# Two heads' k'v in one chain of 128-row matmuls on a block-diagonal v, with v cast by GpSimd and 26 warm-up matmuls

## The chip, the cores and the metric

The kernel runs on one core of one Trainium2 chip. Its engines are TensorE (PE in the profile, with its weight loads as PEld), VectorE (DVE), ScalarE (ACT), GpSimd (POOL) and SyncE (SP), which issues most DMAs. The metric is the device time of one execution in microseconds (us); the median of several runs counts. About 2% of it is a difference that a measurement of this kernel can tell.

## The reference

Eight batches, eight heads, 576 positions, head dimension 64. A linear attention with cosine and sine features is followed by a small token-mixing network on the 512-wide result:

```python
q_p = phi(q, cos_w, sin_w)          # relu(x)*cos, relu(x)*sin: 128 features
k_p = phi(k, cos_w, sin_w)
kv = np.einsum('bhsf,bhsd->bhfd', k_p, v)
z = np.sum(k_p, axis=2)
num = np.einsum('bhsf,bhfd->bhsd', q_p, kv)
den = np.einsum('bhsf,bhf->bhs', q_p, z)[..., None] + 1e-06
x = num / den                       # heads side by side: [B, S, 512]
wq = x @ w_q
wk = x @ w_k
W_tok = scale * np.einsum('bsd,btd->bst', wq, wk)
mixed = np.einsum('bst,btd->bsd', W_tok, x)
out = np.maximum(mixed, 0.0) @ w_out
```

Inputs and output are float32; the kernel's matmuls take bfloat16.

## The kernel before

Everything is unrolled. For each batch, `attention` runs over four pairs of heads, then `moe_front` makes the mixed matrix, and after each second batch `wout` multiplies 1152 rows by w_out and stores them.

A pair of heads is loaded so that head 0 lies on partitions 0 to 63 and head 1 on 64 to 127; each partition holds nine positions (C9 = 9). Loads come in halves of a batch (two pairs), in quarters for the first batch. `kf`, `vf` and `qf` (two buffers each) are the loaded floats. ACT or DVE makes `rk` and `rq` by a relu (line 121) and casts v into `v_ext` (line 116); GpSimd sets a column of ones in `v_ext` (line 119), which gives z beside kv. DVE multiplies `rk` and `rq` by the table `cossin` into `k_p` and `q_p` (line 123).

Per pair PE does two chains of nine matmuls into `kv_ps` (line 136), one per head, each on the 64 partitions of its head, with 128 features as weights and 65 columns of v. `kv_ps` has one bank, and each chain is copied to `kv_sb` (line 144) by ACT or DVE. Between the two chains stand nine transposes of `q_p` into `qpt_ps` (line 147), which DVE copies to `qpt_sb` (line 151). Then ten matmuls give `num_ps` (line 159), DVE takes the reciprocal (line 167) and writes the quotient to `x_sb` (line 168, three buffers).

`moe_front` transposes `x_sb` (`xT_ps`, line 180), multiplies by w_q and w_k (`moe_ps_a`, line 191), transposes a part (`moe_ps_b`), forms `moe_ps_c` (line 213, five matmuls of 512 columns) and `moe_ps_d` (line 226), which ACT or DVE evicts into `mix_sb` (line 233). `wout` fills `moe_ps_e` (line 244), copies it to `o_sb` (line 252) and stores it. All `moe_ps` tiles share three banks.

The order on each engine is made by a scheduler ahead of the run, from the program's order, priorities (`high_priority` for the evictions) and estimated costs; `nc.any` lets it choose between ACT and DVE. It lets the attention of later batches run ahead of the network of earlier ones. Each engine, and SP's queue, then works through its own list in order.

Of the kernel before, what the change touches and what calls it, by code (L numbers as in the profile page):

```python
# [14 lines left out]
FP32 = mybir.dt.float32  # L15
BF16 = mybir.dt.bfloat16
# [6 lines left out]
def kernel(  # L23
# [10 lines left out]
    nc = tc.nc  # L34

    B, H, S, D = q.shape
    DM = H * D
    DH = moe_w_q.shape[1]
    P = 128
    NPAIR = H // 2  # L40
    C9 = (2 * S) // P
# [4 lines left out]
    consts = ctx.enter_context(tc.tile_pool(name="consts", bufs=1))  # L46
    inp = ctx.enter_context(tc.tile_pool(name="inp", bufs=2))
    work = ctx.enter_context(tc.tile_pool(name="work", bufs=2))
    small = ctx.enter_context(tc.tile_pool(name="small", bufs=6))
    xpool = ctx.enter_context(tc.tile_pool(name="xpool", bufs=3))  # L50
    moepool = ctx.enter_context(tc.tile_pool(name="moepool", bufs=2))
    mixpool = ctx.enter_context(tc.tile_pool(name="mixpool", bufs=2))
    outpool = ctx.enter_context(tc.tile_pool(name="outpool", bufs=4))
    psum = ctx.enter_context(tc.tile_pool(name="psum", bufs=1, space=bass.MemoryType.PSUM))

    ident = consts.tile([P, P], BF16)
    make_identity(nc, ident)
# [31 lines left out]
    wo_sb = consts.tile([P, NDM, DM], BF16)  # L89
    nc.vector.tensor_copy(wo_sb, wo_f)  # L90

    num_slices = [(i * P, P) for i in range(4)] + [(S - P, P)]
    cbase_of = [0, 2, 4, 6, 7]
    xread_slices = [(i, 0, P, i * P) for i in range(4)] + [(4, 64, 64, 4 * P)]

    def attention(b, x_sb, nsplit):
        qf = inp.tile([P, NPAIR, C9 * D], FP32, name="qf")
        kf = inp.tile([P, NPAIR, C9 * D], FP32, name="kf")
        vf = inp.tile([P, NPAIR, C9 * D], FP32, name="vf")
        rq = work.tile([P, NPAIR, C9, D], BF16, name="rq")  # L100
        rk = work.tile([P, NPAIR, C9, D], BF16, name="rk")
        q_p = work.tile([P, NPAIR, C9, 2, D], BF16, name="q_p")
        k_p = work.tile([P, NPAIR, C9, 2, D], BF16, name="k_p")
        v_ext = work.tile([P, NPAIR, C9, D + 1], BF16, name="v_ext")

        step = NPAIR // nsplit
        for sp in range(nsplit):
            a, bb = sp * step, (sp + 1) * step
            csb = cossin.unsqueeze(1).to_broadcast([P, step, C9, 2, D])
            for dst, rr, pp, src in ((kf, rk, k_p, k), (vf, None, None, v),  # L110
                                     (qf, rq, q_p, q)):
                s4 = src[b].flatten().rearrange(
                    "(pr p e) -> p pr e", pr=NPAIR, p=P)
                nc.sync.dma_start(dst[:, a:bb, :], s4[:, a:bb, :])
                if rr is None:
                    nc.any.tensor_copy(  # L116
                        v_ext[:, a:bb, :, 0:D],
                        dst[:, a:bb, :].rearrange("p pr (c d) -> p pr c d", c=C9))
                    nc.gpsimd.memset(v_ext[:, a:bb, :, D:D + 1], 1.0)
                else:  # L120
                    nc.any.tensor_scalar(rr[:, a:bb, :, :], dst[:, a:bb, :],  # L121
                                         0.0, None, op0=ALU.max)
                    nc.vector.tensor_mul(  # L123
                        pp[:, a:bb, :, :, :],
                        rr[:, a:bb, :, :].unsqueeze(3).to_broadcast(
                            [P, step, C9, 2, D]),
                        csb)

        for pr in range(NPAIR):
            kv_sb = small.tile([P, 2, D + 1], BF16, name="kv_sb")  # L130
            qpt_ps = psum.tile([P, C9, P], BF16, name="qpt_ps", bufs=1)
            for hh in range(2):
                p0 = hh * 64
                kv_ps = psum.tile([P, D + 1], FP32, name="kv_ps", bufs=1)
                for c in range(C9):
                    nc.tensor.matmul(  # L136
                        kv_ps,
                        k_p[p0:p0 + 64, pr, c, :, :],
                        v_ext[p0:p0 + 64, pr, c, :],
                        start=(c == 0),  # L140
                        stop=(c == C9 - 1),
                    )
                with tc.high_priority(2000):
                    nc.any.tensor_copy(kv_sb[:, hh, :], kv_ps)  # L144
                if hh == 0:
                    for c in range(C9):
                        nc.tensor.transpose(  # L147
                            qpt_ps[:, c, :], q_p[:, pr, c, :, :], ident)
            qpt_sb = small.tile([P, 2, C9, D], BF16, name="qpt_sb")
            with tc.high_priority(2000):  # L150
                nc.vector.tensor_copy(  # L151
                    qpt_sb, qpt_ps.rearrange("f c (hh pp) -> f hh c pp", hh=2))

            for hh in range(2):
                h = 2 * pr + hh
                num_ps = psum.tile([P, SC, D + 1], FP32, name="num_ps", bufs=2)
                for u in range(SC):
                    cb = cbase_of[u]
                    nc.tensor.matmul(  # L159
                        num_ps[:, u, :],  # L160
                        qpt_sb[:, hh, cb:cb + 2, :],
                        kv_sb[:, hh, :],
                        start=True,
                        stop=True,
                    )
                rec = small.tile([P, SC, 1], FP32, name="rec")
                nc.vector.reciprocal(rec, num_ps[:, :, D:D + 1])
                nc.vector.tensor_tensor(  # L168
                    x_sb[:, :, h, :],
                    num_ps[:, :, 0:D],  # L170
                    rec.to_broadcast([P, SC, D]),
                    op=ALU.mult,
                )
# [129 lines left out]
```

## Time and profile before

| | us |
|---|---|
| median of 3 runs | 202.64 |
| fastest and slowest run | 201.63, 207.41 |
| span of the profiled execution | 206.3 |
| PE busy | 168.7 (82%) |
| DVE busy | 136.7 (66%) |
| ACT busy | 101.0 (49%) |
| GpSimd busy | 2.7 (1%) |

The profile is of one execution; for it the page gives the span from the first to the last instruction. Busy times of PE include the latency of its pipeline, so two matmuls that follow each other overlap in the record: what a chain costs is read from the start of one chain to the start of the next. The chain of waits follows the work that ended last backwards from the last instruction. The granted clock is the share of 2.4 GHz that TensorE was given; 0.50 is 1.2 GHz.

### The profile page before, as it was taken

What the parts mean: (1) busy time and instruction counts of PE and PEld (TensorE: products, weight loads), DVE (VectorE), ACT (ScalarE), POOL (GpSimd) and SP (SyncE); (2) the same over time, 40 slices, a digit from 0 to 9 for tenths busy, and PEclk for the clock granted to TensorE, in tenths of its full rate; (3) what the DMA queues carried; (4) which work ended last, traced back from release to release, by engine and by line L of the source; (5) the groups of instructions that cost most, each with busy time, mean ns of one, the idle gap of its engine ahead of it and who ended that gap; (6) DMA issues with size and microseconds to landing.
All of it is one profiled execution on the core that took longest, in us unless ns stands there. A gap on an engine that the chain in (4) does not pass through costs nothing.

```text
span 206.3 us, 4215 instructions
## 1 busy us (share of the span) xinstructions
PE 168.7 (82%) x1696; PEld 102.8 (50%) x1696; DVE 136.7 (66%) x301; ACT 101.0 (49%) x190; POOL 2.7 (1%) x25
## 2 busy tenths in 40 slices
PE   0007889899789999999979999999799999778950
PEld 0006677555445534866645555766554575532420
DVE  1269667945877468978886898878989497723000
ACT  2174579063923645525834858239645434114540
POOL 2000000000000000000000000000000000000000
PEclk9999999999999999999755999999999999965896
DMA  6999999999500028789995066891003870000486
GB/s 189 381 358 332 401 391 391 389 341 327 198 0 2 0 54 201 165 257 394 394 391 216 0 153 147 189 362 72 3 0 80 204 180 2 3 0 0 105 204 149
DMA packets 20514, 39.32 MB, mean 191 GB/s; under 512 B 3088, under 2 KB 3088, under 8 KB 20496
## 3 DMA queue, kind: packets, MB, share of 16 engines
q1 hardware_dynamic: 18912, 37.76, 58.1%
q10 hardware_dynamic: 1584, 1.31, 2.0%
q8 instruction: 13, 0.21, 0.5%
q14 instruction: 5, 0.04, 0.1%
HBM read 29.62 MB, written 9.44 MB: 189 GB/s over the span
## 4 chain that ended last, share of the span: by engine, by line
PE 67%; DVE 10%; DMA 9%; ACT 7%; issue 2%; SPq 1%; POOL 0%; ACTq 0%; DVEq 0%
PE moe_ps_e L244 14%; PE kv_ps L136 12%; PE qpt_ps L147 11%; PE num_ps L159 7%; PE xT_ps L180 6%; DMA kf<-in_k_dram 6%; PE moe_ps_c L213 6%; PE moe_ps_a L191 6%; PE moe_ps_d L226 4%; DMA wq_f<-in_moe_w_q_dram 2%; DVE x_sb L168 2%; ACT mix_sb L233 2%; DVE qpt_sb L151 1%; DVE xT_sb L185 1%; DVE k_p L123 1%
## 5 line engine op out<-in xcount | busy, mean ns | idle before, releaser
L136 PE MATMUL kv_ps<-v_ext,k_p 64*128 64x65 bf16 x576 | 38.5, 211 | 18.9 <-DVE k_p L123 16.3
L136 PEld LDWEIGHTS <-k_p 64*128 64x128 bf16 x576 | 27.7, 106 | 29.1 <-DVE k_p L123 16.3
L244 PE MATMUL moe_ps_e<-wo_sb,mix_sb 128*128 128x512 bf16 x144 | 35.9, 410 | 0.4 <-ACT o_sb L252 0.3
L147 PE MATMUL qpt_ps<-ident,q_p 128*128 128x128 bf16 x288 | 31.8, 254 | 0.2 <-DVE qpt_sb L151 0.2
L168 DVE TENSOR_TENSOR x_sb<-num_ps,rec 128x320 bf16<-128x320 f32 x64 | 30.1, 482 | 0.1
L151 DVE COPY qpt_sb<-qpt_ps 128x1152 bf16<-128x1152 bf16 x32 | 24.2, 756 | 7.0 <-PE qpt_ps L147 6.6
L144 ACT CAST kv_sb<-kv_ps 128x65 bf16<-128x65 f32 x44 | 9.5, 216 | 36.4 <-PE kv_ps L136 35.7
L159 PE MATMUL num_ps<-kv_sb,qpt_sb 128*128 128x65 bf16 x320 | 24.0, 214 | 1.8 <-DVE x_sb L168 1.4
L252 ACT COPY o_sb<-moe_ps_e 128x512 f32<-128x512 f32 x31 | 18.2, 586 | 14.5 <-PE moe_ps_e L244 9.5
L244 PEld LDWEIGHTS <-mix_sb 128*128 128x128 bf16 x144 | 14.7, 104 | 19.1 <-issue 5.6
L147 PEld LDWEIGHTS <-q_p 128*128 128x128 bf16 x288 | 21.1, 113 | 4.1 <-issue 1.7
L180 PE MATMUL xT_ps<-ident,x_sb 128*128 128x128 bf16 (+1 forms) x160 | 19.5, 243 | 4.2 <-DVE x_sb L168 4.2
L121 ACT ACTIVATE rk<-kf 128x1152 bf16<-128x1152 f32 (+1 forms) x17 | 18.4, 1081 | 7.5 <-DMA kf<-in_k_dram 5.7
L123 DVE TENSOR_TENSOR k_p<-rk,cossin 128x2304 bf16<-128x2304 bf16 (+1 forms) x18 | 21.8, 1213 | 0.0
L123 DVE TENSOR_TENSOR q_p<-rq,cossin 128x2304 bf16<-128x2304 bf16 (+1 forms) x18 | 21.8, 1212 | 0.0
L159 PEld LDWEIGHTS <-qpt_sb 128*128 128x128 bf16 x320 | 16.9, 109 | 9.4 <-issue 3.1
L233 ACT ACTIVATE mix_sb<-moe_ps_d 128x64 bf16<-128x64 f32 (+1 forms) x40 | 14.7, 409 | 9.7 <-PE moe_ps_d L226 8.8
L121 ACT ACTIVATE rq<-qf 128x1152 bf16<-128x1152 f32 (+1 forms) x17 | 18.5, 1086 | 1.7 <-DMA qf<-in_q_dram 1.7
L226 PE MATMUL moe_ps_d<-wqkT_sb,kx_sb 64*128 64x512 bf16 x64 | 16.7, 341 | 2.4 <-ACT mix_sb L233 1.5
L233 DVE TENSOR_SCALAR mix_sb<-moe_ps_d 128x512 bf16<-128x512 f32 (+1 forms) x24 | 11.2, 475 | 10.0 <-PE moe_ps_d L226 9.7
L116 ACT CAST v_ext<-vf 128x1152 bf16<-128x1152 f32 (+1 forms) x16 | 17.5, 1103 | 0.0
L180 PEld LDWEIGHTS <-x_sb 128*128 128x128 bf16 (+1 forms) x160 | 12.2, 108 | 10.4 <-DVE x_sb L168 4.7
(40 smaller groups left out, 106.1 us busy)
## 6 DMA issues: line engine op xcount, KB each, us to landing
out_dram<-o_sb SPq DMA_DIRECT2D x72, 128.0 KB, 2.3
kf<-in_k_dram SPq DMA_DIRECT2D x14, 576.0 KB, 10.0
vf<-in_v_dram SPq DMA_DIRECT2D x14, 576.0 KB, 9.4
qf<-in_q_dram SPq DMA_DIRECT2D x14, 576.0 KB, 9.6
kf<-in_k_dram SPq DMA_DIRECT2D x4, 288.0 KB, 5.1
vf<-in_v_dram SPq DMA_DIRECT2D x4, 288.0 KB, 5.7
qf<-in_q_dram SPq DMA_DIRECT2D x4, 288.0 KB, 6.0
wo_f<-in_moe_w_out_dram ACTq DMA_DIRECT2D x1, 1024.0 KB, 9.9
```

Of the source, the lines that this page charges most:

```text
L121: nc.any.tensor_scalar(rr[:, a:bb, :, :], dst[:, a:bb, :], 0.0, None, op0=ALU.max)
L123: nc.vector.tensor_mul(pp[:, a:bb, :, :, :], rr[:, a:bb, :, :].unsqueeze(3).to_broadcast([P, step, C9, 2, D]), csb)
L136: nc.tensor.matmul(kv_ps, k_p[p0:p0 + 64, pr, c, :, :], v_ext[p0:p0 + 64, pr, c, :], start=(c == 0), stop=(c == C9 - 1),)
L147: nc.tensor.transpose(qpt_ps[:, c, :], q_p[:, pr, c, :, :], ident)
L151: nc.vector.tensor_copy(qpt_sb, qpt_ps.rearrange("f c (hh pp) -> f hh c pp", hh=2))
L159: nc.tensor.matmul(num_ps[:, u, :], qpt_sb[:, hh, cb:cb + 2, :], kv_sb[:, hh, :], start=True, stop=True,)
L168: nc.vector.tensor_tensor(x_sb[:, :, h, :], num_ps[:, :, 0:D], rec.to_broadcast([P, SC, D]), op=ALU.mult,)
L180: nc.tensor.transpose(xT_ps[:, j0:j0 + npn], x_sb[p0:p0 + npn, u, 2 * hp:2 * hp + 2, :], ident[p0:p0 + npn, p0:p0 + npn],)
L226: nc.tensor.matmul(mx_ps[:, 0:nn], kx_sb[:, dmc * P:(dmc + 1) * P], wqkT_sb[0:64, n0:n0 + nn], start=True, stop=True,)
L233: nc.any.tensor_scalar(mix_sb[:, dmc, half * S + n0: half * S + n0 + nn], mx_ps[:, 0:nn], scale_moe, 0.0, op0=ALU.mult, op1=ALU.max,)
L244: nc.tensor.matmul(o_ps, mix_sb[:, dmc, rt * P:(rt + 1) * P], wo_sb[:, dmc, :], start=(dmc == 0), stop=(dmc == NDM - 1),)
L252: nc.any.tensor_copy(o_sb, o_ps)
```

## The change

v of a pair is laid out as a block-diagonal matrix: a tile `v_buf0` or `v_buf1` (by the batch's parity) has, for each pair and position, 2 x 65 columns; a head's 64 partitions hold its v and a one in its own 65 columns and zeros in the other head's. Zeros and ones are set once, ahead of the loop, by DVE for the first 64 partitions and by GpSimd for the others. Each v is cast into its block by GpSimd, 64 partitions and one pair at a time (eight casts of 64x576 per batch). One chain of nine matmuls over all 128 partitions, with 130 columns, then gives both heads' kv, and one copy of 128x130 evacuates it. The transposes of q follow the chain in the program. 26 matmuls of 512 columns on a tile of ones open PE's program. `xpool` has two buffers instead of three, and `rq` and `rk` one instead of two.

```diff
-    xpool = ctx.enter_context(tc.tile_pool(name="xpool", bufs=3))
+    xpool = ctx.enter_context(tc.tile_pool(name="xpool", bufs=2))
...
+    warm = consts.tile([P, 512], BF16)
+    nc.vector.memset(warm, 1.0)
+    warm_ps = psum.tile([P, 512], FP32, name="warm_ps", tag="moe", bufs=3)
+    for _ in range(26):
+        nc.tensor.matmul(warm_ps, warm[:, 0:P], warm, start=True, stop=True)
...
+    v_bufs = []
+    for i in range(2):
+        vb = consts.tile([P, NPAIR, C9, 2, D + 1], BF16, name=f"v_buf{i}")
+        for hh in range(2):
+            p0 = hh * 64
+            eng = nc.vector if hh == 0 else nc.gpsimd
+            eng.memset(vb[p0:p0 + 64, :, :, 1 - hh, :], 0.0)
+            eng.memset(vb[p0:p0 + 64, :, :, hh, D:D + 1], 1.0)
+        v_bufs.append(vb)
...
-        rq = work.tile([P, NPAIR, C9, D], BF16, name="rq")
-        rk = work.tile([P, NPAIR, C9, D], BF16, name="rk")
+        rq = work.tile([P, NPAIR, C9, D], BF16, name="rq", bufs=1)
+        rk = work.tile([P, NPAIR, C9, D], BF16, name="rk", bufs=1)
...
-        v_ext = work.tile([P, NPAIR, C9, D + 1], BF16, name="v_ext")
+        v_ext = v_bufs[b % 2]
...
-                    nc.any.tensor_copy(
-                        v_ext[:, a:bb, :, 0:D],
-                        dst[:, a:bb, :].rearrange("p pr (c d) -> p pr c d", c=C9))
-                    nc.gpsimd.memset(v_ext[:, a:bb, :, D:D + 1], 1.0)
+                    for hh in range(2):
+                        p0 = hh * 64
+                        for pr in range(a, bb):
+                            nc.gpsimd.tensor_copy(
+                                v_ext[p0:p0 + 64, pr, :, hh, 0:D],
+                                dst[p0:p0 + 64, pr, :].rearrange(
+                                    "p (c d) -> p c d", c=C9))
...
-            for hh in range(2):
-                p0 = hh * 64
-                kv_ps = psum.tile([P, D + 1], FP32, name="kv_ps", bufs=1)
-                for c in range(C9):
-                    nc.tensor.matmul(
-                        kv_ps,
-                        k_p[p0:p0 + 64, pr, c, :, :],
-                        v_ext[p0:p0 + 64, pr, c, :],
-                        start=(c == 0),
-                        stop=(c == C9 - 1),
-                    )
-                with tc.high_priority(2000):
-                    nc.any.tensor_copy(kv_sb[:, hh, :], kv_ps)
-                if hh == 0:
-                    for c in range(C9):
-                        nc.tensor.transpose(
-                            qpt_ps[:, c, :], q_p[:, pr, c, :, :], ident)
+            kv_ps = psum.tile([P, 2, D + 1], FP32, name="kv_ps", bufs=1)
+            for c in range(C9):
+                nc.tensor.matmul(
+                    kv_ps,
+                    k_p[:, pr, c, :, :],
+                    v_ext[:, pr, c, :, :],
+                    start=(c == 0),
+                    stop=(c == C9 - 1),
+                )
+            with tc.high_priority(2000):
+                nc.any.tensor_copy(kv_sb, kv_ps)
+            for c in range(C9):
+                nc.tensor.transpose(
+                    qpt_ps[:, c, :], q_p[:, pr, c, :, :], ident)
```

The scheduler makes a new order for the changed program. At the beginning of DVE's list, before the first multiplications, stood this:

```order
L84 CAST wqk_sb<-wq_f 128x4x64
L121 TENSOR_SCALAR rk<-kf 128x576
L85 CAST wqk_sb<-wk_f 128x4x64
L116 CAST v_ext<-vf 128x9x64
L121 TENSOR_SCALAR rq<-qf 128x576
L116 CAST v_ext<-vf 128x9x64
L90 CAST wo_sb<-wo_f 128x2048
```

And now:

```order
L57 MEMSET warm 128x512
L104 MEMSET v_buf_144 64x36x65
L90 CAST wqk_sb<-wq_f 128x4x64
L105 MEMSET v_buf_144 64x36
L91 CAST wqk_sb<-wk_f 128x4x64
L104 MEMSET v_buf_149 64x36x65
L105 MEMSET v_buf_149 64x36
L140 TENSOR_SCALAR rq<-qf 128x576
L96 CAST wo_sb<-wo_f 128x2048
```

Five memsets took the place of the first relu of k, which went to ACT, and of two casts of v, which went to GpSimd.

On ACT, the place where `moe_ps_d` of the first batch is evicted (names with their buffer numbers) read, before:

```order
L233 ACTIVATE mix_sb_372<-moe_ps_d_431 128x512
L121 ACTIVATE rk_1184<-kf_1181 128x1152
L144 CAST kv_sb_641<-kv_ps_663 128x65
L233 ACTIVATE mix_sb_372<-moe_ps_d_440 128x64
L233 ACTIVATE mix_sb_372<-moe_ps_d_446 128x64
L116 CAST v_ext_1187<-vf_1182 128x18x64
L233 ACTIVATE mix_sb_372<-moe_ps_d_452 128x64
```

and now:

```order
L161 CAST kv_sb_605<-kv_ps_607 128x130
L249 ACTIVATE mix_sb_366<-moe_ps_d_425 128x512
L249 ACTIVATE mix_sb_366<-moe_ps_d_431 128x512
L249 ACTIVATE mix_sb_366<-moe_ps_d_434 128x64
L249 ACTIVATE mix_sb_366<-moe_ps_d_437 128x512
L249 ACTIVATE mix_sb_366<-moe_ps_d_440 128x64
L249 ACTIVATE mix_sb_366<-moe_ps_d_443 128x512
L249 ACTIVATE mix_sb_366<-moe_ps_d_446 128x64
```

Seven of the batch's eight evictions now stand in a row on ACT, where four stood among other casts and relus. In the whole program ACT has 29 of the 32 evictions of 512 columns (19 before), DVE three (13 before). On PE the first real instructions are now the nine transposes of the first pair, then its kv chain; before, the first kv chain stood ahead of them.

## Rows read from the trace of the kernel before

**Rows 1.** The chain that ended last: shares of the span by engine, by line.

```profile
PE 67%; DVE 10%; DMA 9%; ACT 7%; issue 2%; SPq 1%; POOL 0%; ACTq 0%; DVEq 0%
PE moe_ps_e L244 14%; PE kv_ps L136 12%; PE qpt_ps L147 11%; PE num_ps L159 7%; PE xT_ps L180 6%; DMA kf<-in_k_dram 6%; PE moe_ps_c L213 6%; PE moe_ps_a L191 6%; PE moe_ps_d L226 4%; DMA wq_f<-in_moe_w_q_dram 2%; DVE x_sb L168 2%; ACT mix_sb L233 2%; DVE qpt_sb L151 1%; DVE xT_sb L185 1%; DVE k_p L123 1%
```

**Rows 2.** Stretches: length, busy PE, PEld, DVE, ACT, POOL (instructions), clock, DMA, GB/s.

```profile
16.30:76.50 60.20, 54.77 (x477) 34.74 (x478) 42.90 (x92) 31.46 (x51) 0.52 (x4) 1.00 0.65 236
114.00:182.60 68.60, 63.67 (x760) 39.54 (x755) 55.49 (x124) 35.43 (x82) 0.52 (x4) 1.00 0.41 105
```

**Rows 3.** The chain in order of time: start, length, moe_ps_c's five matmuls.

```profile
64.87 2.41 PE moe_ps_c L213 x5
...
109.98 2.41 PE moe_ps_c L213 x5
...
136.30 1.31 PE moe_ps_c L213 x5
```

**Rows 4.** kv_ps alone on PE: stretch, length, busy (matmuls), clock, DMA, GB/s.

```profile
16.00:76.50 60.50, 14.80 (x189) 1.00 0.65 236
100.40:114.00 13.60, 2.19 (x35) 0.50 0.83 309
```

**Rows 5.** PE in order of time: start, length, engine, line, matmuls.

```profile
19.66 0.68 PE L136 MATMUL kv_ps<-v_ext,k_p 64*128 64x65 bf16 x9
20.27 1.14 PE L147 MATMUL qpt_ps<-ident,q_p 128*128 128x128 bf16 x9
21.34 0.67 PE L136 MATMUL kv_ps<-v_ext,k_p 64*128 64x65 bf16 x9
...
143.79 0.46 PE L136 MATMUL kv_ps<-v_ext,k_p 64*128 64x65 bf16 x9
144.18 0.68 PE L147 MATMUL qpt_ps<-ident,q_p 128*128 128x128 bf16 x9
144.69 0.32 PE L159 MATMUL num_ps<-kv_sb,qpt_sb 128*128 128x65 bf16 x5
```

**Rows 6.** Waits: who waited for whom, us in total, times, longest.

```profile
ACT rk L121 <- DVE k_p L123: 1.8, 1, 1.8
...
PE kv_ps L136 <- ACT kv_sb L144: 1.4, 4, 0.4
```

**Rows 7.** Groups by shape: line, engine, operation, count | busy us, mean ns | idle before.

```profile
L123 DVE TENSOR_TENSOR k_p<-rk,cossin 128x2304 bf16<-128x2304 bf16 x14 | 18.8, 1345 | 0.0
...
L116 ACT CAST v_ext<-vf 128x1152 bf16<-128x1152 f32 x14 | 16.2, 1165 | 0.0
...
L233 ACT ACTIVATE mix_sb<-moe_ps_d 128x512 bf16<-128x512 f32 x19 | 11.4, 604 | 8.9 <-PE moe_ps_d L226 8.3 <-PE kv_ps L136 0.5
...
L233 DVE TENSOR_SCALAR mix_sb<-moe_ps_d 128x512 bf16<-128x512 f32 x13 | 9.0, 689 | 2.0 <-PE moe_ps_d L226 1.8
...
masks.py:199 POOL TENSOR_SCALAR_AFFINE_SELECT ident<-ident 128x128 bf16<-128x128 bf16 x1 | 0.3, 292 | 0.0
...
masks.py:197 POOL MEMSET ident<- 128x128 bf16 x1 | 0.2, 204 | 0.3 <-POOLq L287 0.3
...
L287 POOL MEMSET const-bfloat16-1.0<- 128x1 bf16 x1 | 0.1, 101 | 0.0
```

**Rows 8.** The chain in order of time: the first of two casts of v.

```profile
85.53 1.05 ACT v_ext L116
```

**Rows 9.** DVE and PE in order of time at the start, columns as in rows 5.

```profile
11.69 1.23 DVE L90 CAST wo_sb<-wo_f 128x2048 bf16<-128x2048 f32 x1 [0.30 <-DMA wo_f<-in_moe_w_out_dram]
...
16.18 0.75 DVE L123 TENSOR_TENSOR q_p<-rq,cossin 128x1152 bf16<-128x1152 bf16 x1
...
16.32 0.67 PE L136 MATMUL kv_ps<-v_ext,k_p 64*128 64x65 bf16 x9 [16.32 <-DVE k_p L123]
```

**Rows 10.** Stretches of 1 us at the end, columns as in rows 2.

```profile
198.00:199.00 1.00, 0.84 (x4) 0.20 (x2) 0.00 (x0) 0.33 (x1) 0.00 (x0) 1.00 0.91 205
...
202.00:203.00 1.00, 0.00 (x0) 0.00 (x0) 0.00 (x0) 0.00 (x0) 0.00 (x0) 0.88 0.88 201
```

## The prediction

> **What bounds the kernel now.** I read the chain of waits first. TensorE (PE) holds 67% of it, VectorE (DVE) 10%, transfers 9%, ScalarE (ACT) 7% [rows 1]. The chain's largest lines are moe_ps_e (14%), kv_ps (12%), which is what the change rewrites, and qpt_ps (11%) [rows 1]. Then the long stretches: from 16.3 to 76.5 us PE is busy 54.77 of 60.20 us, from 114 to 182.6 us 63.67 of 68.60; DVE is busy 42.90 and 55.49 in them, ACT 31.46 and 35.43 [rows 2]. So PE's stream sets the pace, DVE is close behind, ACT and the DMA engines (share 0.65 and 0.41) have room.
>
> Then TensorE's clock. The same five matmuls of moe_ps_c take 2.41 us at 64.87 and at 109.98, and 1.31 us at 136.30 [rows 3]. At 109.98 the granted clock reads 0.50, that is 1.2 GHz [rows 4]; at 136.30 it reads 1.00, 2.4 GHz [rows 2]. At 64.87 it also reads 1.00 [rows 2], but the duration is that of 1.2 GHz, so I take the first 60 us of matmuls as run at 1.2 GHz: the record begins too late to show it. Of the 64 kv chains (nine matmuls each) 189 matmuls fall before 76.5 us and 35 between 100.4 and 114 us [rows 4]: 224 of 576, 12 of the 32 head pairs at 1.2 GHz and 20 at 2.4.
>
> **The kv chain.** A pair now costs two chains of nine 65-column matmuls, afterwards one of nine with 130 columns. Start to start, nine of the old ones take 20.27 - 19.66 = 0.61 us at 1.2 GHz and 144.18 - 143.79 = 0.39 us at 2.4 GHz [rows 5]. The trace has no 130-column matmul; the nearest is the transpose chain, nine loads of 128x128 weights and nine matmuls of 128 columns: 21.34 - 20.27 = 1.07 us and 144.69 - 144.18 = 0.51 us [rows 5]. So a pair saves 2 x 0.61 - 1.07 = 0.15 us at 1.2 GHz, less 0.02 for two more columns, and 2 x 0.39 - 0.52 = 0.26 us at 2.4 GHz; I take 0.23, because such chains often stand between others. That is 12 x 0.13 + 20 x 0.23 = 1.6 + 4.6 = 6.2 us, all from PE's stream. The bounds are 0 (time goes by columns, of which there are as many as before) and 12 x 0.15 + 20 x 0.27 = 7.2 us.
>
> [...]
>
> **Evacuations.** 64 copies of 128x65 become 32 of 128x130, and the second chain of a pair no longer waits until the one kv_ps bank is copied out. PE waited 1.4 us for kv_sb on ACT [rows 6]. The transposes now stand between one pair's chain and the next: -1.4 us (bounds 0 and 1.4).
>
> **v leaves ACT.** ACT loses 14 casts of 1165 ns and two smaller [rows 7]. Most lie beside PE's work. Two of them, at 85.5 and 86.7 us, are on the chain with 1.05 us each [rows 8]: -2.1 us (bounds 0 and 2.1).
>
> **v on GpSimd.** 64 casts of 64x576. No such cast is in the trace. GpSimd's nearest rows are a memset of 128 elements, 204 ns against 101 ns for one element (0.81 ns per element), and an affine select of 128, 292 ns (1.5 ns per element) [rows 7]. That makes 576 elements 0.57 to 0.97 us; I take 0.8. Eight per batch are 6.4 us, where a batch takes about (182.6 - 16.3) / 8 = 20.8 us: GpSimd keeps up, and it would set the pace only from 2.6 us per cast. Behind a waiting cast only other casts queue; the DMA of vf two batches on waits for them, and SP's later kf and qf with it, covered by the DMA engines' idle share. At 0 us.
>
> **What the scheduler moved.** The 512-wide mix_sb evictions stood 19 on ACT at 604 ns and 13 on DVE at 689 [rows 7]; now 29 stand on ACT. Ten more over eight batches are 10 / 8 x 0.604 = 0.76 us more per batch on one engine, behind each other, where two engines shared them; moe_ps_d waits for it, but PE has transposes and num_ps between, so the price is between 0 and 8 x 0.76 = 6 us, and I take 2. rk and rq have one buffer each: rk of the next batch waits for the last k_p multiplication of this one, and kv_sb and mix_sb queue behind it on ACT. ACT had one such wait, 1.8 us [rows 6]; between 0 and 7 x 1.8 = 13 us, I take 1, since the product mostly stands well ahead. x_sb with two buffers: num_ps of a batch stands behind the front of the batch two before it in PE's order, so 0.
>
> **The start.** DVE gets five memsets, the largest two of 2340 elements; at the rate of the cast of w_out, 2048 elements in 1.23 us, these are 1.4 us each, and if three times that, 4.2. They stand ahead of that cast, which cannot start before its transfer lands at 11.69 us [rows 9], and DVE gave up two casts of v and a relu there. So q_p is done at 16.18 + 0.75 = 16.93 us [rows 9] as before, through the same cast, cosines and table. PE now begins with the transposes, which need q_p, not with kv at 16.32 [rows 9]: 0.6 us later, with the first pair 0.13 us shorter: +0.5.
>
> **The warm-up.** 26 matmuls of 512 columns at 0.26 to 0.48 us each (moe_ps_c's rows, 1.31 / 5 and 2.41 / 5 [rows 3]) last 6.8 to 12.5 us. They start after one memset of 512 elements, by the rate above under a microsecond, so they end between 8.5 and 14.5 us; PE was idle there until 16.3, so they delay nothing. Nor do they help: the first real matmul comes at 17, 2.5 to 8.5 us later. At the kernel's end PE stops before 199 and the granted clock falls between 202 and 203 us [rows 10], after some 4 us of idleness. A gap under 4 us needs nearly all 26 at 1.2 GHz, and then there was no high clock to keep. At 0.
>
> **Sum.** -6.2 - 1.4 - 2.1 + 2 + 1 + 0.5 = -6.2 us. The profiled execution has a span of 206.3 us; the page gives no other time for it, and of the three runs only the slowest, 207.41, is longer than that. 206.3 - 6.2 = 200.1 us of span. The median of the runs, 202.64, lies 3.7 below the profiled span, and I take the difference from it: 196.4. I predict **196 us**. With every gain at its upper bound and no cost but the start, it is 202.6 - 10.7 + 0.5 = 192; with mix_sb and rk bare in every batch it is 196 + 4 + 12 = 212, which needs every one of these waits to have no product or matmul beside it.
>
> **Rivals.**
> First, the clock rises earlier: the warm-up's level holds, or chains with fewer pauses lift it before the first moe_ps_e. For: five microseconds of the first stretch are idle, and the denser chains fill some of it. Against: the gap above, and that PE was already 91% busy there without a rise [rows 2]. If all of the stretch ran at 2.4 GHz, DVE would hold it: the fast stretch is 68.6 / 55.49 = 1.24 times its DVE time, so 42.90 x 1.24 = 53, less 2 for kv copies, 51 us instead of 60: about 9 us more, 187; half of it 191.
>
> Second, the chain saves nothing, because time goes by columns: 0.78 us per pair stays, and the 6.2 us drop out of the sum: 202.5 us. For it: every old matmul moves half the columns of a new one. Against it: 43 ns for 65 columns and 57 for 128 [rows 5], so columns are not the whole price. [...]
>
> Third, slower: GpSimd's casts and DVE's k_p and q_p multiplications hold each other up. The place is each of the 16 half batches, where four casts in a row (3.2 us) follow the same transfers as the multiplications of 1345 ns [rows 7]. 6.6 half batches fall into the fast stretch (16 x 68.6 / 166.3). DVE's 55.49 us lose about 4 there (mix_sb and kv_sb), and PE would need about 65.5, so DVE has 14 us of room, and the rival decides from 2.1 us of waiting per half batch. If the multiplications wait out the whole burst, 6.6 x 3.2 = 21 us, this stretch grows by 7 us and the one from 76.5 to 114 by its share, 4: some 207 us. Waits half as long stay hidden. No row shows GpSimd and DVE at work on large tiles together. [...]
>
> **Chances.** Forecast (192.5 to 199.5) 0.47; earlier clock (186 to 192) 0.20; chain saves nothing (200 to 205) 0.20; DVE and GpSimd collide, or the ACT waits lie bare (204 to 212) 0.13. About 2%, 4 us, is what a measurement of this kernel tells from no change; the three runs lie 201.63 to 207.41. Faster than 198.6: three quarters of the first, all of the second, a quarter of the third: 0.60. Slower than 206.7: four fifths of the last, 0.11. Between: 0.29. Eight in ten lie between **185 and 206**; the forecast's own range is 192.5 to 199.5.
>
> **What would show it.** Right: kv_ps x288 with nine in about 1.07 or 0.51 us start to start; its share of the chain at 10% or less; no v cast on ACT; GpSimd's casts under 1 us; k_p still at 1345 ns; first transposes near 17 us; moe_ps_c before the first moe_ps_e still at 2.41 us. Wrong: k_p and q_p means above 1.6 us (third rival); nine kv matmuls near 0.78 us (second); moe_ps_c at 1.31 us before 60 us (first); or waits of PE for mix_sb of over 4 us.

## The result and the profile after

The changed kernel takes 179.45 us (median of 4 runs, 178.11 to 180.15) where the kernel before takes 203.03 (4 runs, 201.63 to 207.41): a ratio of 0.886, 95% interval 0.879 to 0.892. The prediction was 196 us with a range of 185 to 206. Its sign was right; the gain of 24 us is more than three times the 6.6 it forecast, and the time lies below the range. Run again on another chip, the same kernel took 180.5 us beside 208.15 for the one before (0.861, 0.853 to 0.869).

The profiled run took 179.77 us, its span is 178.0. The profiled execution of before is a slow one: its span of 206.3 us is longer than three of the four runs took, and the two profiles lie 28.3 us apart where the medians lie 24 apart. First the page's busy times and its chain of waits by engine and by line:

```profile
PE 147.2 (83%) x1434; PEld 90.6 (51%) x1434; DVE 134.1 (75%) x279; ACT 89.9 (51%) x167; POOL 56.6 (32%) x75
...
PE 56%; DVE 17%; ACT 10%; DMA 8%; issue 4%; SPq 1%; POOL 0%; ACTq 0%
PE moe_ps_e L260 10%; PE kv_ps L153 10%; PE qpt_ps L163 9%; PE moe_ps_d L242 6%; PE moe_ps_c L229 5%; PE xT_ps L196 5%; PE num_ps L175 5%; DMA qf<-in_q_dram 5%; DVE k_p L142 5%; PE moe_ps_a L207 4%; DVE q_p L142 3%; DVE qpt_sb L167 3%; DVE x_sb L184 3%; ACT wqkT_sb L214 2%; DMA wq_f<-in_moe_w_q_dram 2%
```

PE's share of the chain fell from 67% to 56% [rows 1], its busy time from 168.7 to 147.2 us, of which the warm-up is some 8.6; DVE's share rose from 10% to 17% with nearly the same busy time. DVE is now the second limit.

Where the time went is seen best stage by stage. The four bursts of `wout` (moe_ps_e) cut the span into stages. Columns as in rows 2. Of before:

```profile
16.30:72.10 55.80, 50.37 (x467) 33.12 (x468) 39.88 (x85) 29.34 (x49) 0.52 (x4) 1.00 0.69 252
72.10:117.00 44.90, 42.63 (x459) 26.25 (x459) 35.40 (x79) 24.54 (x45) 0.51 (x4) 0.85 0.74 238
117.00:155.20 38.20, 36.01 (x438) 22.62 (x439) 32.98 (x71) 22.52 (x49) 0.52 (x4) 1.00 0.46 125
155.20:189.40 34.20, 30.25 (x302) 17.11 (x301) 21.64 (x54) 12.55 (x31) 0.00 (x0) 0.90 0.31 71
```

And of after:

```profile
18.80:62.20 43.40, 36.46 (x411) 26.31 (x412) 39.00 (x83) 21.59 (x38) 27.43 (x32) 0.86 0.84 310
62.20:96.90 34.70, 33.14 (x362) 21.17 (x362) 31.18 (x64) 22.16 (x43) 9.00 (x12) 1.00 0.77 240
96.90:130.90 34.00, 32.72 (x354) 20.78 (x352) 30.95 (x64) 20.52 (x41) 8.95 (x12) 1.00 0.69 210
130.90:161.10 30.20, 26.91 (x251) 15.44 (x252) 20.46 (x54) 12.84 (x28) 0.00 (x0) 0.99 0.34 80
```

The first stage lost 12.4 us, but it starts 2.5 us later; the second lost 10.2, the third 4.2, the fourth 4.0; the last takes 16.9 in both. The third stage is granted 1.00 in both kernels: there the 4.2 us don't come from the clock, but about 0.5 of them are nine transposes that stand in another stage in after. The first two lost more, and in them the clock differs. In before, moe_ps_e's matmuls of 512 columns start 216 ns apart where 1.00 is granted and 426.5 ns apart at 0.50 (medians of 118 and 8 cases), about 2.4 and 1.2 columns a nanosecond; 2.4 and 1.2 GHz stand for these two levels. The same view of after, in stretches of 1 us:

```profile
8.00:9.00 1.00, 1.00 (x6) 0.44 (x5) 1.00 (x3) 0.00 (x0) 0.00 (x0) 1.00 0.94 295
14.00:15.00 1.00, 0.00 (x0) 0.00 (x0) 0.80 (x3) 0.98 (x2) 0.80 (x2) 0.51 0.94 323
25.00:26.00 1.00, 0.57 (x10) 0.48 (x8) 1.00 (x2) 0.40 (x2) 0.27 (x2) 1.00 1.07 396
32.00:33.00 1.00, 0.71 (x7) 0.71 (x8) 1.00 (x5) 0.00 (x0) 1.00 (x2) 0.50 1.06 394
38.00:39.00 1.00, 0.46 (x9) 0.29 (x7) 0.66 (x1) 0.81 (x3) 0.94 (x2) 1.00 1.07 396
```

The warm-up lifts the granted clock to 1.00 (2.4 GHz; its own matmuls start 427 ns apart up to 7 us and 216 ns apart from 7.3), it is back at 0.50 by 14.5 us while PE is idle, rises and falls once more with the first pairs, and from 38 us reads 1.00 until 160. In the kernel before it rose at 76.5 us and fell again from 100.4 to 114 [rows 4]. moe_ps_c's five matmuls, in the chain's order of time, confirm the early rise: 1.31 us already in the first batch, where before still has 2.41 in the second batch, at 64.87 [rows 3].

```profile
40.03 1.31 PE moe_ps_c L229 x5
```

### The profile page after: what moved, and what is told of

Read it like the earlier page. It is cut to its first block, busy times and chain, and to the rows that moved or that the text cites. A ratio compares the mean times of both kernels' runs of the same rounds, so it can differ in the third digit from the quotient of the medians.

```text
span 178.0 us, 3706 instructions
## 1 busy us (share of the span) xinstructions
PE 147.2 (83%) x1434; PEld 90.6 (51%) x1434; DVE 134.1 (75%) x279; ACT 89.9 (51%) x167; POOL 56.6 (32%) x75
## 3 DMA queue, kind: packets, MB, share of 16 engines
q10 hardware_dynamic: 1584, 1.31, 2.5%
## 4 chain that ended last, share of the span: by engine, by line
PE 56%; DVE 17%; ACT 10%; DMA 8%; issue 4%; SPq 1%; POOL 0%; ACTq 0%
PE moe_ps_e L260 10%; PE kv_ps L153 10%; PE qpt_ps L163 9%; PE moe_ps_d L242 6%; PE moe_ps_c L229 5%; PE xT_ps L196 5%; PE num_ps L175 5%; DMA qf<-in_q_dram 5%; DVE k_p L142 5%; PE moe_ps_a L207 4%; DVE q_p L142 3%; DVE qpt_sb L167 3%; DVE x_sb L184 3%; ACT wqkT_sb L214 2%; DMA wq_f<-in_moe_w_q_dram 2%
## 5 line engine op out<-in xcount | busy, mean ns | idle before, releaser
L135 POOL CAST v_buf<-vf 64x576 bf16<-64x576 f32 x64 | 51.2, 822 | 71.9 <-DMA vf<-in_v_dram 33.4
L163 PE MATMUL qpt_ps<-ident,q_p 128*128 128x128 bf16 x288 | 29.8, 228 | 10.5 <-DVE q_p L142 9.4
L260 PE MATMUL moe_ps_e<-wo_sb,mix_sb 128*128 128x512 bf16 x144 | 33.9, 391 | 0.3
L153 PE MATMUL kv_ps<-v_buf,k_p 128*128 128x130 bf16 x288 | 29.0, 235 | 2.0 <-ACT kv_sb L161 0.8
L163 PEld LDWEIGHTS <-q_p 128*128 128x128 bf16 x288 | 19.1, 102 | 14.9 <-DVE q_p L142 10.7
L175 PE MATMUL num_ps<-kv_sb,qpt_sb 128*128 128x65 bf16 x320 | 21.3, 196 | 3.0 <-DVE x_sb L184 1.5
L142 DVE TENSOR_TENSOR k_p<-rk,cossin 128x2304 bf16<-128x2304 bf16 (+1 forms) x18 | 23.3, 1297 | 0.2 <-ACT rk L140 0.2
L153 PEld LDWEIGHTS <-k_p 128*128 128x128 bf16 x288 | 19.7, 105 | 5.3 <-ACT kv_sb L161 1.7
L249 ACT ACTIVATE mix_sb<-moe_ps_d 128x512 bf16<-128x512 f32 (+1 forms) x50 | 19.3, 441 | 5.1 <-PE moe_ps_d L242 4.7
L161 ACT CAST kv_sb<-kv_ps 128x130 bf16<-128x130 f32 x24 | 6.4, 268 | 28.0 <-PE kv_ps L153 28.0
L196 PE MATMUL xT_ps<-ident,x_sb 128*128 128x128 bf16 (+1 forms) x160 | 17.4, 220 | 1.3 <-DVE x_sb L184 1.1
L201 DVE COPY xT_sb<-xT_ps 128x576 bf16<-128x576 bf16 x32 | 13.4, 441 | 2.4 <-PE xT_ps L196 2.2
```

What stands on the lines that cost most here:

```text
L135: nc.gpsimd.tensor_copy(v_ext[p0:p0 + 64, pr, :, hh, 0:D], dst[p0:p0 + 64, pr, :].rearrange("p (c d) -> p c d", c=C9))
L142: nc.vector.tensor_mul(pp[:, a:bb, :, :, :], rr[:, a:bb, :, :].unsqueeze(3).to_broadcast([P, step, C9, 2, D]), csb)
L153: nc.tensor.matmul(kv_ps, k_p[:, pr, c, :, :], v_ext[:, pr, c, :, :], start=(c == 0), stop=(c == C9 - 1),)
L163: nc.tensor.transpose(qpt_ps[:, c, :], q_p[:, pr, c, :, :], ident)
L175: nc.tensor.matmul(num_ps[:, u, :], qpt_sb[:, hh, cb:cb + 2, :], kv_sb[:, hh, :], start=True, stop=True,)
L196: nc.tensor.transpose(xT_ps[:, j0:j0 + npn], x_sb[p0:p0 + npn, u, 2 * hp:2 * hp + 2, :], ident[p0:p0 + npn, p0:p0 + npn],)
```

## The experiments

Five theories stand in the expectations. **A**: the merged chain lifts the clock, and the warm-up is useless. **B**: the warm-up brings the clock forward. **C**: v's leaving ACT is the larger part. **D**: each change of the number of rows between two matmuls costs PE about 95 ns, and the 64-row chains are full of such changes. **E**: the number of matmuls, weight loads and evacuations is the price.

### The warm-up

e1_no_warm is the changed kernel without it.

```diff
-    warm = consts.tile([P, 512], BF16)
-    nc.vector.memset(warm, 1.0)
-    warm_ps = psum.tile([P, 512], FP32, name="warm_ps", tag="moe", bufs=3)
-    for _ in range(26):
-        nc.tensor.matmul(warm_ps, warm[:, 0:P], warm, start=True, stop=True)
```

> The changed kernel without the memset and the 26 warm-up matmuls; nothing else differs. Theory A (the merged chain lifts the clock, the warm-up is over 8 us before the first real matmul and does nothing): 178 to 182 us, against 179.5 of the changed kernel, with the clock risen for good before 45 us. Theory B (the warm-up is what brings the clock forward): 190 to 197 us, with matmuls at 1.2 GHz until the first moe_ps_e near 65 us.

Measured: 180.44 us (179.59 to 182.56), ratio 0.896 (0.884 to 0.907); the changed kernel has 179.45 and 180.5 on other chips. Its granted clock rises at 25.0, falls at 31.8 and rises for good at 35.2 us, some 2.7 us before the changed kernel's. The warm-up does nothing here.

e2_before_warm26 and e3_before_warm60 are the kernel before with these same lines added, with 26 and with 60 matmuls.

> The kernel before with the memset and the 26 warm-up matmuls ahead of it. Theory A: 200 to 205 us, as before (203), since the level falls again before the first kv chain at 16 us. Theory B: 188 to 194 us, with the first moe_ps_e near 62 us instead of 72.

> The kernel before with 60 warm-up matmuls, which at the two levels seen last until about 15 to 17 us, so that the first kv chain meets the full clock. It prices the clock alone, with the old chains. If the clock of the first 60 us is worth about half of the gain: 189 to 194 us, first moe_ps_e near 61 us. If DVE or the transfers would hold that stretch anyway: 200 to 204 us. [...]

Measured: e2 200.24 us (196.75 to 203.05, 10 runs; before on this chip 206.66), ratio 0.984 (0.973 to 0.995); e3 205.51 (199.44 to 212.11, 10 runs), ratio 0.995 (0.987 to 1.004). Stretches of e2, then of e3, columns as in rows 2:

```profile
20.00:46.00 26.00, 24.06 (x238) 16.68 (x239) 18.89 (x41) 14.24 (x22) 0.27 (x2) 0.50 1.04 390
47.00:53.00 6.00, 4.12 (x59) 2.84 (x57) 4.63 (x9) 5.52 (x10) 0.26 (x2) 1.00 0.88 302
54.00:60.00 6.00, 5.68 (x58) 4.04 (x57) 5.16 (x11) 3.60 (x5) 0.00 (x0) 0.50 0.37 145
```

```profile
18.00:22.00 4.00, 0.39 (x8) 0.31 (x5) 4.00 (x7) 2.55 (x3) 0.00 (x0) 1.00 1.01 376
24.00:49.00 25.00, 23.61 (x257) 17.78 (x254) 17.11 (x42) 12.98 (x20) 0.26 (x2) 0.50 1.02 376
50.00:56.00 6.00, 5.08 (x71) 3.21 (x70) 5.29 (x16) 4.45 (x10) 0.26 (x2) 1.00 0.75 276
```

These traces show what that of before left open: with 64-row chains PE really works at 1.2 GHz from 20 to 46 us, 24 of 26 us busy. And when the level is held into the first pairs (e3), PE has 0.39 us of work from 18 to 22 us and the level is gone for the next 25. The short warm-up gives the old chains 1.6%, less than the 2% that a measurement of this kernel can tell; the long one has no measurable effect.

e6_after_warm60 is the changed kernel with `range(60)`.

> The changed kernel with 60 warm-up matmuls instead of 26, so that TensorE is at work until the first pair. Theory A (the order and density of the real chains set the level): the level is lost again within the first batch, 177 to 181 us. Theory B (a level carried into the work stays): no low stretch after 19 us, where the changed kernel has some 14 us at 1.2 GHz; that is worth 4 to 7 us: 172 to 176 us.

Measured: 184.04 us (183.52 to 186.91), ratio 0.884 (0.877 to 0.891), 3.5 us slower than the changed kernel on the same chip. Both theories missed it. The clock was as B wanted, 2.4 GHz until 23.3 us; but ACT had the relu of the next half batch ahead of the first kv_sb, and that relu waited for DVE's k_p. ACT, then PE, in order of time, with the idle time before and its releaser in brackets:

```profile
22.27 1.16 ACT L140 ACTIVATE rk<-kf 128x1152 bf16<-128x1152 f32 x1 [4.29 <-DVE k_p L142]
23.34 0.25 ACT L161 CAST kv_sb<-kv_ps 128x130 bf16<-128x130 f32 x1
```

```profile
23.74 1.13 PE L153 MATMUL kv_ps<-v_buf,k_p 128*128 128x130 bf16 x9 [4.11 <-ACT kv_sb L161]
```

PE idled 4.1 us, the level fell (the granted clock reads 1.00 from 22 to 23 us, 0.50 from 24 to 25), and this wait is the one that `rk`'s single buffer makes. It accounts for little of the slower time, though: e6's first burst of `wout` starts at 62.5 us, after's at 62.2 and e10's, the changed kernel on e6's chip, at 61.5. Most of the 3.5 us is lost later, and why stays open. Nor does the run tell what a level held without a gap would be worth.

### The chain

e4_two_chains takes only the merged chain out of the changed kernel: two 64-row chains, as before, on the block-diagonal tile.

```diff
-            kv_ps = psum.tile([P, 2, D + 1], FP32, name="kv_ps", bufs=1)
...
+            for hh in range(2):
+                p0 = hh * 64
+                kv_ps = psum.tile([P, D + 1], FP32, name="kv_ps", bufs=1)
...
+                        k_p[p0:p0 + 64, pr, c, :, :],
+                        v_ext[p0:p0 + 64, pr, c, hh, :],
...
+                    nc.any.tensor_copy(kv_sb[:, hh, :], kv_ps)
```

> The changed kernel (warm-up, GpSimd's casts into the block-diagonal tile, fewer buffers) with the two old chains of 64 rows and 65 columns per pair and their two evacuations. It prices the chain. Theory A: 195 to 201 us, with the clock low until the first moe_ps_e, because the chain carried both the stream and the clock. Rival C (v off ACT is the larger part): 184 to 190 us. By the prediction's price of the stream alone, 6.2 us, it would be 186.

Measured: 200.21 us (198.32 to 201.97, 4 runs; before on this chip 206.66, and e2 200.24). Everything in the change but the chain, that is v on GpSimd, the buffers, the new schedule and the later start, moves nothing in sum against a kernel that only has the warm-up; single parts may cancel. C falls, as far as old chains go; the chain, with its copies, carries some 20 us (e1 on the same chip: 180.44).

e8_two_chains_128 parts D from E: still two chains of 65 columns with two copies, but each over all 128 rows (the zeros of the block-diagonal tile make it the same sum).

```diff
-                        k_p[p0:p0 + 64, pr, c, :, :],
-                        v_ext[p0:p0 + 64, pr, c, hh, :],
+                        k_p[:, pr, c, :, :],
+                        v_ext[:, pr, c, hh, :],
```

> The changed kernel with two chains per pair again, each of nine matmuls with 65 columns and its own evacuation, but over all 128 partitions (the block-diagonal tile supplies the zeros): as many matmuls, weight loads and copies as the kernel with two 64-row chains (200 us), other rows. Theory D (a matmul costs PE some 95 ns more where it follows one with another number of rows, and the old 64-row chains pay that at their ends and wherever the order chops them): 180 to 185 us. Theory E (the number of matmuls, weight loads and evacuations is the price): 196 to 202 us.

Measured: 188.72 us (188.42 to 191.67), ratio 0.926 (0.923 to 0.929). With the same number of matmuls, loads and copies as e4, 11.5 us are gone by the medians, on two chips (9.9 between the fastest runs of each). PE of e8, in order of time:

```profile
122.01 0.44 PE L154 MATMUL kv_ps<-v_buf,k_p 128*128 128x65 bf16 x9
122.30 0.27 PE L165 MATMUL qpt_ps<-ident,q_p 128*128 128x128 bf16 x2
...
129.37 0.44 PE L154 MATMUL kv_ps<-v_buf,k_p 128*128 128x65 bf16 x9
129.65 0.31 PE L177 MATMUL num_ps<-kv_sb,qpt_sb 128*128 128x65 bf16 x5
```

Nine 65-column matmuls take 0.28 to 0.29 us from start to start; on 64 rows they took 0.39 [rows 5]. The neighbours pay as well. Transposes of before, followed by a 64-row chain, and of after, followed by a 128-row chain:

```profile
128.23 0.51 PE L147 MATMUL qpt_ps<-ident,q_p 128*128 128x128 bf16 x6
128.67 0.46 PE L136 MATMUL kv_ps<-v_ext,k_p 64*128 64x65 bf16 x9
129.06 0.53 PE L180 MATMUL xT_ps<-ident,x_sb 128*128 128x128 bf16 x5
```

```profile
70.98 0.55 PE L163 MATMUL qpt_ps<-ident,q_p 128*128 128x128 bf16 x7
71.37 0.63 PE L153 MATMUL kv_ps<-v_buf,k_p 128*128 128x130 bf16 x8
```

Six take 0.44 us ahead of 64 rows, seven take 0.39 ahead of 128. Worked out from the starts of all matmuls in the traces, median time from one start to the next at 2.4 GHz:

| matmul | next has as many rows | next has another number of rows |
|---|---|---|
| 65 columns, 64 rows (before, 114 to 182 us) | 33 ns (190 cases) | 125 ns (12, before a transpose) |
| transpose, 128 rows (before, same) | 56 ns (95) | 152 ns (14, before kv) |
| num_ps, 65 columns, 128 rows (before, same) | 29 ns (120) | 126 ns (9, before kv) |
| 130 columns, 128 rows (after, 38 to 160 us) | 59 ns (183) | 153 ns (11, before moe_ps_d) |
| 65 columns, 128 rows (e8, 61 to 160 us) | 30 ns (298) | 129 ns (13, before moe_ps_d) |

A change of the number of rows costs 92 to 99 ns at 2.4 GHz, in either direction. At 1.2 GHz (before, 16 to 76 us) it is 55 against 173 ns for kv and 106 against 247 for the transposes: 118 to 141 ns. The traces have 229 such changes in before, 234 in e2, 228 in e4, 162 in e8 and 170 in after. A wait for another engine isn't the reason: inside the five transposes of one `xT_ps`, four over 128 rows and the last over 64, the step from the fourth to the fifth takes 151 ns, the others 56 (16 cases, before, 114 to 182 us).

Rows aren't the whole rule. `moe_ps_c` has weights of 64 columns, and a transpose that stands ahead of its first matmul, which has 128 rows as well, takes 149 ns instead of 56 (six cases, after, 38 to 160 us). So there a change of the weights from 128 columns to 64 costs 93 ns, about as much; before and after have 16 of these each, half or more of them together with a change of rows.

Does the clock have a part in the 11.5 us? The second and third stages of e4, then of e8, hold the same work; columns as in rows 2:

```profile
69.00:109.80 40.80, 39.22 (x461) 25.11 (x461) 34.47 (x77) 21.94 (x46) 12.76 (x16) 0.92 0.73 233
109.80:147.50 37.70, 36.19 (x424) 22.43 (x422) 32.38 (x67) 21.79 (x47) 6.30 (x8) 1.00 0.49 142
```

```profile
67.60:105.10 37.50, 35.66 (x462) 23.19 (x461) 34.40 (x77) 21.79 (x46) 13.57 (x16) 1.00 0.79 254
105.10:141.20 36.10, 34.01 (x424) 21.50 (x422) 32.30 (x67) 21.74 (x47) 6.27 (x8) 1.00 0.52 149
```

In the third stage, at 2.4 GHz in both, e8 is 1.6 us shorter with 26 changes fewer (70 and 44): rows alone. In the second, where e4 is granted 0.92, it is 3.3 us shorter with 18 fewer. Over the first two stages e4 is granted 0.50 for 32.8 us, e8 for 13.6. Changing the rows alone thus brought the clock's rise forward as well.

e7_two_copies keeps the merged chain and copies its result out in two halves. It was run twice, the second time (e11) beside the changed kernel (e10).

```diff
-                nc.any.tensor_copy(kv_sb, kv_ps)
+                for hh in range(2):
+                    nc.any.tensor_copy(kv_sb[:, hh, :], kv_ps[:, hh, :])
```

> The changed kernel with two copies of 128x65 per pair instead of one of 128x130. It prices the evacuation alone. Theory D: 179 to 182 us. If the 32 saved copies and the waits for them are a large part of the gain: 184 us or more.

> The changed kernel itself, on the same chip as the three kernels beside it. All theories: 178 to 181 us. If it comes out 4 us or more higher, what earlier runs on other chips showed of a few us (two copies instead of one, all matmuls on 128 rows) has to be read against this run and not against the first one.

> The merged chain of nine 130-column matmuls with its result copied out by two 128x65 copies instead of one of 128x130. Theory D (the matmuls' row counts are the price): within 2 us of the changed kernel, since PE's stream is the same. Theory E (the single kv_ps bank and the copy that frees it are a price of their own): 4 to 8 us slower, with PE's wait for kv_sb growing from under 1 us in all to several, or the copies holding ACT up ahead of rk.

Measured: e7 186.79 us, ratio 0.917 (0.913 to 0.920); e11 186.17 (185.4 to 188.22), ratio 0.898 (0.890 to 0.906), beside e10's 180.5 (179.16 to 182.39), ratio 0.861 (0.853 to 0.869). There are two results. Merging the columns at equal rows gives 188.72 - 186.79 = 1.9 us (e8 and e7 ran on one chip). And the second copy costs 186.17 - 180.5 = 5.7 us (6.2 between the fastest runs of each), as E expected. The three steps, rows, merging and copies, add up to 19.1 us, about the 20 of the chain. Of the two ways that E named, PE's wait for kv_sb is not enough: in e11 it is 1.9 us in all, as the view of waits has it (in total, times, longest), against 0.8 in after:

```profile
PE kv_ps L153 <- ACT kv_sb L162: 1.9, 4, 0.6
```

```profile
PE kv_ps L153 <- ACT kv_sb L161: 0.8, 2, 0.4
```

The copies themselves, by shape, of e11 and then of after (count | busy us, mean ns | idle before):

```profile
L162 ACT CAST kv_sb<-kv_ps 128x65 bf16<-128x65 f32 x54 | 11.7, 216 | 33.4 <-PE kv_ps L153 31.4 <-DVE kv_sb L162 1.1
```

```profile
L161 ACT CAST kv_sb<-kv_ps 128x130 bf16<-128x130 f32 x24 | 6.4, 268 | 28.0 <-PE kv_ps L153 28.0
```

Of 268 ns for 130 columns, 216 remain for 65: half the columns save 52 ns, so by estimate 164 of the 216 (216 - 52) don't go by columns, and ACT is busy 5.3 us longer. That is about the loss, but ACT is busy only half of the span, and which of its instructions came late by it stays open: e11's profiled run was granted 0.95 in its fast stretches and e7's 0.75, so their stages can't be laid against those of after.

### v on GpSimd, and all matmuls on 128 rows

e5_v_any lets the scheduler place the casts of v; it put 61 of 64 on ACT.

```diff
-                            nc.gpsimd.tensor_copy(
+                            nc.any.tensor_copy(
```

> The changed kernel with the 64 casts of v left to the scheduler's choice of engine, not to GpSimd. It prices GpSimd's part. If GpSimd's share is small: 179 to 184 us. If the changed kernel needs ACT and DVE free, 64 casts of about 0.7 us on them cost 45 us of engine time and 8 to 20 us of the run: 188 to 200 us.

Measured: 190.4 us (188.6 to 191.04), ratio 0.934 (0.923 to 0.945), 10 to 11 us above the changed kernel. The casts, and DVE's multiplications, by shape:

```profile
L135 ACT CAST v_buf<-vf 64x576 bf16<-64x576 f32 x61 | 39.2, 675 | 4.0 <-DMA vf<-in_v_dram 3.5
...
L142 DVE TENSOR_TENSOR k_p<-rk,cossin 128x2304 bf16<-128x2304 bf16 x14 | 18.7, 1337 | 0.0
```

On ACT the new layout's casts cost 39.2 us of busy time, more than twice the 16.2 of the old one's full-width casts [rows 7]. So with the block-diagonal layout, v on ACT costs some 10 us; this doesn't say that v on ACT cost the kernel before 10 us.

e9_all_128 goes one step further than the change: every matmul on 128 rows, by zeros in the weights of moe_ps_c and full tiles elsewhere. e12_all128_no_warm is the same without the warm-up.

```diff
+        wb = consts.tile([P, SC, 2 * DH], BF16, name=f"wkj_buf{i}")
+        nc.gpsimd.memset(wb, 0.0)
...
-        wk_ps = psum.tile([P, SC, DH], BF16, name="moe_ps_b", tag="moe", bufs=3)
+        wk_ps = psum.tile([P, SC, 2 * DH], BF16, name="moe_ps_b", tag="moe", bufs=3)
...
-                wqkT_sb[64:128, j0:j0 + nj],
-                ident[64:128, 64:128],
+                wqkT_sb[:, j0:j0 + nj],
+                ident,
...
-        kx_ps = psum.tile([64, DM], FP32, name="moe_ps_c", tag="moe", bufs=3)
+        kx_ps = psum.tile([P, DM], FP32, name="moe_ps_c", tag="moe", bufs=3)
...
-                    wqkT_sb[0:64, n0:n0 + nn],
+                    wqkT_sb[:, n0:n0 + nn],
```

> The changed kernel with every other 64-row matmul made one of 128 rows too: the last slice of the x transposes taken over all 128 rows, the second transpose over both halves of wqkT, the weights of moe_ps_c zero-padded to 128 columns (a persistent tile, evicted in two copies) and its last slice to 128 rows, so that moe_ps_d runs over 128 rows with zeros below. The changed kernel's trace shows 170 changes of the row count between neighbouring matmuls. Theory D: up to 170 x 0.095 = 16 us of PE's stream, of which DVE (134 us busy of 178) may leave half: 168 to 176 us. Theory E: 179 to 183 us, since nothing is shorter in columns and one copy per batch is added.

> Every matmul on 128 rows, without the warm-up matmuls and their memset. Theory A (the warm-up changes nothing): 174 to 176 us as with them. Theory B (the warm-up brings the clock forward): 178 us or more.

Measured: e9 174.94 us (174.66 to 175.22), ratio 0.859 (0.856 to 0.862); e12 174.37 (174.0 to 177.2), ratio 0.838 (0.831 to 0.844), 6 us below the changed kernel on the same chip. Both beat it, D holds for the other matmuls too, and the warm-up is again worth nothing. Their traces have no change of rows or of columns left. At 95 ns each, the 170 changes of rows are 16 us; PE's busy time fell by 11.4 (139.0 in e1, 127.6 in e12), and only 6 us show in the end. The stages of e12 tell why:

```profile
59.80:95.00 35.20, 31.57 (x368) 21.49 (x367) 33.60 (x72) 20.01 (x40) 11.09 (x14) 1.00 0.84 269
95.00:129.00 34.00, 31.77 (x370) 21.75 (x370) 32.40 (x71) 21.25 (x40) 9.43 (x12) 1.00 0.60 176
129.00:156.70 27.70, 23.85 (x226) 14.03 (x224) 18.30 (x51) 12.00 (x27) 0.00 (x0) 1.00 0.37 87
```

The second and third stages are as long as in after; DVE is busy 33.6 of 35.2 and 32.4 of 34 us in them. DVE hardly ever rests there, which makes it the likely bound. The fourth stage, where it has room, lost 2.5 us.

## Why the prediction was wrong

**The step that failed is the kv chain.** Its term was 6.2 us (0.13 us a pair at 1.2 GHz, 0.23 at 2.4), with 7.2 as its bound. Measured by themselves, the rows gave 11.5 us (e4 to e8; with 206.66 and 206.75 us for before on the two chips) and the merging 1.9, together 13.4. The term took the chain's own stream, at an unchanged clock, for the whole price.

The stream itself was misread. The prediction took 0.39 us for nine old matmuls [rows 5] and spread it as 43 ns over each. In fact eight of them cost 33 ns and the ninth 125, because a matmul on 128 rows comes next. And it priced the new chain, at 1.2 GHz, by transposes that stood ahead of a 64-row chain and so carried a change of rows in their 1.07 us. The new chain's own time was right, 1.07 us (19.76 to 20.83) and 0.95 (21.82 to 22.77) at 1.2 GHz, and 0.53 (69.33 to 69.86) at 2.4. It never asked what a neighbour pays: a 64-row chain between 128-row matmuls costs once on the way in (96 to 97 ns in the table) and once on the way out (92).

What PE's stream gained is an estimate: from e4 to e7 the changes fell by 70 (228 and 158), which is 6.7 us at 95 ns, and by the medians above the merged columns give 1.5, about 8 us together. That 6.2 lies near this is luck: the 0.39 us held one change for each of the 64 chains, and the prediction didn't know of it. Two for each would be 128, but changes came back elsewhere, where the network's 64-row matmuls now stand among 128-row ones: at the kv chains there are 35 in after instead of 120, between other matmuls 26 more. The likely rest of the 13.4, some 5 us, is the clock, which the prediction left where it was.

The second rival was half right. Where the number of rows stays, a matmul of 65 columns takes 29 to 33 ns in the traces and one of 130 takes 59: there time does go by columns, and merging them saves next to nothing, 1.9 us from e8 to e7. The gain came with the rows (11.5 us, e4 to e8) and the copies (5.7 us, e11 to e10).

**The evacuations** were the second term of the wrong size: 1.4 us, bounded at PE's own wait for kv_sb [rows 6]; e11 against e10 gives 5.7. An evacuation was priced by the wait that the trace shows on PE, and not by what it takes from ACT. How it comes to 5.7 us stays open.

**The clock** rose early, as the first rival had it (a chance of 0.20, 186 to 192 us). Of its two reasons, chains with fewer pauses fit e1, where no warm-up is left and the level still rises at 25 and for good at 35 us; the warm-up's level does not fit. No run tells the fewer pauses from the fuller rows. That rival said DVE would hold the stretch to 76.5 us at 51 us; DVE was busy 39.0 of the 43.4 us of the first stage of after, 90%. Rival and forecast were treated as apart, but e4 to e8 shows both coming from the rows: fewer changes, and 13.6 instead of 32.8 us at 1.2 GHz. Adding what was predicted for the two gives 187 us; of the 7.5 us that are missing to 179.45, the evacuations account for 4.3, and no run divides the rest. How the 24 us divide between cheaper chains and more time at 2.4 GHz stays open too: e4 to e8 is 66 changes fewer, 6.3 us at 95 ns each, and measures 11.5, and the clock's earlier rise is the likely rest, but no run held the work and moved the clock alone.

**v leaves ACT, v on GpSimd, the scheduler's moves and the start** together were +1.4 us; e4 against e2 has 0.0. In single points: the cast took 822 ns, where 0.8 us was taken. By shape, of after:

```profile
L135 POOL CAST v_buf<-vf 64x576 bf16<-64x576 f32 x64 | 51.2, 822 | 71.9 <-DMA vf<-in_v_dram 33.4 <-PE qpt_ps L163 28.0 <-PE kv_ps L153 5.4
...
L142 DVE TENSOR_TENSOR k_p<-rk,cossin 128x2304 bf16<-128x2304 bf16 x14 | 19.6, 1398 | 0.2 <-ACT rk L140 0.2
...
L249 ACT ACTIVATE mix_sb<-moe_ps_d 128x512 bf16<-128x512 f32 x29 | 17.0, 598 | 5.0 <-PE moe_ps_d L242 4.7
```

The third rival, GpSimd against DVE, is real but small: k_p at 1398 ns instead of 1345 [rows 7], well short of the 1.6 us that was to show it deciding. ACT's 29 evictions of mix_sb came as the order said, and the view of PE's waits lists none for them: the +2 was not needed. rk's single buffer cost ACT 5.6 us of waiting instead of 1.8 [rows 6], which stayed hidden in after; in e6 it made PE wait 4.1 us.

**The start** was wrong in its reason. PE's first real matmul came at 18.83 us, not near 17. DVE at the start of after, then GpSimd:

```profile
16.55 1.07 DVE L142 TENSOR_TENSOR k_p<-rk,cossin 128x1152 bf16<-128x1152 bf16 x1
17.55 1.22 DVE L142 TENSOR_TENSOR q_p<-rq,cossin 128x1152 bf16<-128x1152 bf16 x1
18.69 0.75 DVE L142 TENSOR_TENSOR k_p<-rk,cossin 128x1152 bf16<-128x1152 bf16 x1
```

```profile
16.35 1.81 POOL L135 CAST v_buf<-vf 64x576 bf16<-64x576 f32 x2 [0.78 <-DMA vf<-in_v_dram]
```

The cast of w_out that stands ahead came 0.9 us later with its transfer, and the first two multiplications took 1.07 and 1.22 us beside GpSimd's casts, 0.75 once these were over. That is some 2 us, where +0.5 was taken.

**The warm-up** was right: it ended at 10.1 us, within the 8.5 to 14.5 forecast, the level fell before the first real matmul, and e1 has the same time without it.

## What to carry to other kernels

Read a chain's cost together with its neighbours: split the start-to-start times by whether the next matmul has the same number of rows before dividing by the count. Where 64-row and 128-row matmuls alternate, filling the unused rows with zeros can be worth more than halving the matmuls: here 11.5 us (e4 to e8) against 1.9 (e8 to e7). Look whether the next engine has room for it: in the second and third stages of e12, with DVE busy 95% of both, the last step brought nothing, in the fourth 2.5 us. A copy out of PSUM can cost more than the wait that PE shows for it: here 5.7 us, where that wait grew by 1.1.

## What the runs showed of the hardware

- A change of the number of rows between two matmuls costs 92 to 99 ns at 2.4 GHz and 118 to 141 ns at 1.2 GHz, into 64 rows and out of them (before, e8 and after); a change from 128 to 64 columns of weights costs 93 ns at 2.4 GHz (after). What PE does in that time no run shows.
- GpSimd and DVE took longer on some large tiles beside each other. In after, DVE's multiplication of 128x1152 took 1.07 and 1.22 us instead of 0.75 beside a cast, and a cast of 128x256 ahead of it 1.47 us (at 4.49 us) instead of the 0.29 of before, while GpSimd wrote a memset of 64x2340 that lasted 2.18 us. GpSimd's pair of casts took 1.81 us beside these multiplications, 1.40 at 11.33 us with DVE idle for most of it, and 1.40 at 6.21 us too, with DVE writing a memset for most of it. The runs show the durations, not the cause. Over the whole kernel the mean of k_p rose by 4% only (1345 to 1398 ns).
- ACT's copy of 128x130 took 268 ns, that of 128x65 216 ns.
